# RWKV-7 recurrence and Wave-MLP mixer on one core: all transposes as 64-row halves into PSUM bank pairs, with merged evictions, products and stores, one bank pool and a new order

## The chip, the cores and the metric

One NeuronCore of a Trainium2 chip runs the kernel. Times are device microseconds of one execution. The kernel before has a median of 204.11 us over 3 runs (203.92 to 204.88). The engines are PE (TensorE, matmuls and transposes), ACT (ScalarE), DVE (VectorE), POOL (GpSimd) and SP (SyncE, which issues most transfers). Each engine runs its own instructions in a fixed order and waits on semaphores for the others.

## The reference

Four batches of 768 steps, 8 heads of 40 features (320 in all). First a recurrence over the steps, for each head, then a mixer over the whole sequence of a batch.

```python
for t in range(S):                       # state: [B, H, D, D]
    y[:, :, t] = einsum('bhd,bhde->bhe', rt, state)
    Sa = einsum('bhde,bhe->bhd', state, at)
    state = state * wt[:, :, None, :] - einsum('bhd,bhe->bhde', Sa, bt) \
            + einsum('bhd,bhe->bhde', vt, kt)
...
theta = x @ w_theta                      # x = y as [B, S, 320]
zr, zi = x * cos(theta), x * sin(theta)
y = einsum('ts,bsd->btd', w_tok_r, zr) + einsum('ts,bsd->btd', w_tok_i, zi)
u = x + y
out = u + maximum(u @ w_ch, 0.0)
```

## The kernel before, in words

**Tiles.** The steps are cut into 24 tiles of 128 steps, six to a batch, tile `i` of batch `i // 6`. A tile holds all 8 heads, as 4 pairs of heads padded from 40 to 64 features, so that a pair fills 128 columns (and, turned, 128 partitions).

**Preparation of a tile (`prep`).** SP loads w, k, b, a, v and r. ACT takes the logarithm of w (L426). PE sums it over the steps (`cs`, L436 and L439: the sums up to and with each step, and the tile's total per head); ACT takes the Exp (L443). The factor that leaves out the step itself comes in two ways: for the first 7 tiles from a second matmul and a second Exp (L449, L452), after that from an addition on DVE (`wi`, L455) and an Exp from SBUF (L460). k, b and a are multiplied by these factors, one `product` each (L409 on DVE, L410 on POOL). PE turns k and b (8 transposes of 128x128 into one PSUM bank), a (4) and v (4) with an identity as the moving operand (`transpose_pairs`, L373); ACT copies the result to SBUF as 32-bit words (L376) or DVE as 16-bit halves (L379). r, and v of the first 8 tiles, come in runs of eight steps for two tiles at a time (`turn_runs`, L504, L508).

**Scores.** Four sets per tile (`psi`, `phi`, `lamv`, `lamu`): 8 matmuls of 64 rows each (L532), two per head pair, into a pair of banks, then one eviction of 1024 columns with the triangular mask: on DVE (L542), or as an ACT copy (L544) and a POOL select (L546).

**Recurrence and readout.** `x0` (L573, L579), its copy `nx`, `nu` (L591) and its copy, both through ACT; then the new state `gt` (L612). For tiles 1 to 3 of the first batch PE adds the old state (L607) and DVE scales the sum (L631); from tile 4 on (`FROM_POOL = 4`) DVE adds (L623) and POOL scales (L627). The state and `nu` are turned by PE as well. `y` (L718 to L727) is scaled by DVE into `x` (L734).

**Mixer.** `theta` turns x of two tiles (L656), multiplies by `w_theta` (L688, and L698 for the 64 features left of each tile, both tiles side by side), and copies each tile's theta by ACT (L753). `sines` makes cosine and sine by ACT (L773) and one product each, `zr` and `zi` (L787 on DVE, L788 on POOL). `mix_row` adds up 12 matmuls a tile (L801) over the token weights, which were turned by PE earlier (L869, L874, L876); DVE adds x (L808). `channels` turns u, multiplies by `w_ch`, and DVE makes the output (L824), which SP stores tile by tile (L827). For a second tile of a pair the two weights are needed shifted by 64 rows; PE makes these copies by shifted identities in `wide` (L847, evicted at L851).

**Order and PSUM.** Every step is added to a plan with `add`. The order of all 1614 steps is the list `ORDER`; `HOMES` gives each PSUM result its bank; `PICK` names the steps that go to their second engine. Four of the eight banks form two pairs (`ps_d`), used for the scores; the other four are single banks (`ps_s`), used for all else. `WARM` puts 45 idle matmuls at the start (L920). A matmul that uses 64 rows and one that uses 128 are different row modes of PE.

Of the kernel before, what the change touches and what calls it, by code (L numbers as in the profile page):

```python
# [18 lines left out]
DOUBLE = 4  # L19
FROM_POOL = 4  # L20
EXCLUSIVE = 7
RUNS = 8
ORDER = [
# [184 lines left out]
def kernel(  # L208
# [52 lines left out]
    def paired(t):  # L261
        return t.rearrange("p (g c) d -> p g c d", c=2)
# [418 lines left out]
    def mixed(kind, q, lhs, wt, wkeys, lkey, at="tile"):  # L681
# [11 lines left out]
        if alone(q):  # L693
            return
# [263 lines left out]
```

## Time and profile before

| | |
|---|---|
| runs | 203.92, 204.11, 204.88 us |
| the profiled execution's span | 206.2 us |
| PE matmuls: instructions, busy | 3355, 193.7 us |
| DVE, ACT, POOL busy | 171.0, 154.3, 135.4 us |
| transferred | 30.82 MB, mean 149 GB/s |
| scores' masked eviction on DVE (L542) | 86 of 1217 to 1220 ns |
| the same as an ACT copy (L544), with a POOL select (L546) | 10 of 1023 to 1044 ns, 10 of 1087 to 1091 ns |
| transposes' evictions on ACT, 256 and 512 words (L376) | 375 to 386 and 590 ns |
| transposes' evictions on DVE, 512 and 1024 halves (L379) | 420 and 688 ns |
| Exp: 328 columns (L443), and the second one (L452, L460) | 24 of 454 ns, and 7 of 442, 17 of 476 ns |
| product of 320 columns on POOL (L410) and on DVE (L409) | 814 to 865 ns, 484 to 488 ns |

Busy time of an engine counts each moment once, so where successive instructions overlap it is less than count times mean. Matmuls are pipelined: one takes a latency of 180 to 300 ns, but the next starts long before it ends, so a busy PE can hold more or less work. The granted clock is given as a share of full speed; in this execution it is 1.00 in every stretch. "<-" with an engine and a line after an idle time names what ended it.

### The profile page before, as it was taken

The page shows a single profiled execution, that of the slowest core. Times are in us where ns is not written, and L with a number is a line of the kernel's source. Part 1 is how long each engine was busy: PE and PEld are TensorE (multiplying, and loading weights), DVE is VectorE, ACT ScalarE, POOL GpSimd, SP SyncE. Part 2 cuts the span into 40 slices and gives each one's busy share as a digit, 9 for nine tenths or more (in the row PEclk, how much of TensorE's full clock was granted, in tenths as well). Part 3 has the DMA queues.
Part 4 walks back from the last instruction along what each step waited for, and adds up shares of the span by engine and source line. Part 5 has one row for each costly group of instructions (what it writes and reads, how often), then busy time and mean ns, then how long its engine had stood idle before and what let it go on. Part 6 is the DMA issues. An engine that isn't in the chain of part 4 may idle for free. (4 is left out here: it accounts for less than half of the span.)

```text
span 206.2 us, 8107 instructions
## 1 busy us (share of the span) xinstructions
PE 193.7 (94%) x3355; PEld 155.8 (76%) x3355; DVE 171.0 (83%) x267; ACT 154.3 (75%) x345; POOL 135.4 (66%) x200
## 2 busy tenths in 40 slices
PE   6798999989898999999989999999999999999993
PEld 6586877877786788778768787989788877876761
DVE  4369988979998999799888889999999988867353
ACT  3377888879998989998877678799998955784001
POOL 8318545859896999687449949675399891339100
PEclk9999999999999999999999999999999999999999
DMA  6989977988999999999999799979898010100222
GB/s 107 212 139 242 168 132 152 189 150 195 185 193 167 185 164 186 199 164 217 166 234 157 149 197 168 170 161 185 166 199 213 15 59 5 64 3 33 99 95 95
DMA packets 127013, 30.82 MB, mean 149 GB/s; under 512 B 117632, under 2 KB 126976, under 8 KB 126976
## 3 DMA queue, kind: packets, MB, share of 16 engines
q1 hardware_dynamic: 124544, 27.54, 67.1%
q0 software_dynamic: 2432, 2.77, 8.4%
q8 instruction: 26, 0.43, 0.9%
q14 instruction: 11, 0.09, 0.2%
HBM read 29.13 MB, written 3.93 MB: 160 GB/s over the span
## 5 line engine op out<-in xcount | busy, mean ns | idle before, releaser
L410 POOL TENSOR_TENSOR kb<-raw_kb,ex 128x320 bf16<-128x320 f32 x46 | 36.9, 814 | 19.3 <-ACT ex L443 6.9
L801 PE MATMUL ps_s<-zr,wtok_r 128*128 128x320 bf16 x144 | 40.8, 299 | 1.0 <-ACT wtok_r L876 1.0
L801 PE MATMUL ps_s<-zi,wtok_i 128*128 128x320 bf16 x144 | 40.7, 299 | 0.0
L542 DVE TENSOR_TENSOR phi<-ps_d,mask_n 128x1024 bf16<-128x1024 f32 x23 | 28.0, 1218 | 5.1 <-PE ps_d L532 5.0
L542 DVE TENSOR_TENSOR psi<-ps_d,mask_p 128x1024 bf16<-128x1024 f32 x23 | 28.1, 1220 | 2.4 <-PE ps_d L532 1.4
L542 DVE TENSOR_TENSOR lamu<-ps_d,mask_p 128x1024 bf16<-128x1024 f32 x23 | 27.9, 1218 | 2.5 <-PE ps_d L532 1.7
L788 POOL TENSOR_TENSOR zi<-cs,xp 128x320 bf16<-128x320 f32 x21 | 16.6, 802 | 10.0 <-ACT cs L773 10.0
L410 POOL TENSOR_TENSOR ah<-raw_a,we 128x320 bf16<-128x320 f32 x23 | 19.9, 865 | 4.7 <-DMA raw_a<-in_a_dram 1.8
L542 DVE TENSOR_TENSOR lamv<-ps_d,mask_p 128x1024 bf16<-128x1024 f32 x17 | 20.6, 1217 | 1.5 <-PE ps_d L532 1.4
L801 PEld LDWEIGHTS <-wtok_r 128*128 128x128 bf16 x144 | 14.0, 97 | 5.7 <-ACT wtok_r L876 1.2
L532 PE MATMUL ps_d<-aT,kbT 64*128 64x128 bf16 x384 | 17.1, 221 | 0.5 <-ACT aT L376 0.5
L788 POOL TENSOR_TENSOR zr<-cs,xp 128x320 bf16<-128x320 f32 x19 | 15.3, 820 | 2.3 <-ACT cs L773 2.3
L373 PE MATMUL ps_s<-wide,kb 128*128 128x128 bf16 x192 | 15.7, 223 | 1.1 <-POOL kb L410 1.0
L801 PEld LDWEIGHTS <-wtok_i 128*128 128x128 bf16 x144 | 14.1, 98 | 3.6
L627 POOL TENSOR_TENSOR gt<-sum,ex 128x320 bf16<-128x320 f32 x13 | 9.6, 737 | 10.3 <-DVE sum L623 7.6
L508 ACT COPY rT<-ps_s 128x512 bf16<-128x512 bf16 x24 | 13.4, 598 | 3.1 <-PE ps_s L504 1.8
L808 DVE TENSOR_TENSOR up<-ps_s,xp 128x320 bf16<-128x320 f32 x22 | 10.6, 487 | 5.8 <-PE ps_s L801 5.7
L532 PEld LDWEIGHTS <-kbT 64*128 64x128 bf16 x384 | 12.5, 96 | 3.3 <-issue 1.3
L725 PE MATMUL ps_s<-kb,lamv 128*128 128x40 bf16 x192 | 14.8, 180 | 0.0
L727 PE MATMUL ps_s<-kb,lamu 128*128 128x40 bf16 x192 | 14.7, 179 | 0.0
L443 ACT ACTIVATE ex<-ps_s 128x328 f32<-128x328 f32 x24 | 10.9, 454 | 4.4 <-PE ps_s L439 3.1
L373 PEld LDWEIGHTS <-kb 128*128 128x128 bf16 x192 | 11.9, 99 | 3.0 <-POOL kb L410 1.6
(168 smaller groups left out, 600.3 us busy)
## 6 DMA issues: line engine op xcount, KB each, us to landing
raw_w<-in_w_dram SPq DMA_DIRECT2D x24, 160.0 KB, 4.2
raw_kb<-in_b_dram SPq DMA_DIRECT2D x24, 160.0 KB, 4.0
raw_kb<-in_k_dram SPq DMA_DIRECT2D x24, 160.0 KB, 3.8
raw_a<-in_a_dram SPq DMA_DIRECT2D x24, 160.0 KB, 4.2
raw_v<-in_v_dram SPq DMA_DIRECT2D x24, 160.0 KB, 3.7
raw_r<-in_r_dram SPq DMA_DIRECT2D x24, 160.0 KB, 3.9
out_dram<-oo SPq DMA_DIRECT2D x24, 160.0 KB, 1.9
wrow_i<-in_moe_w_tok_i_dram POOLq DMA_DIRECT2D x6, 192.0 KB, 5.9
```

What stands on the lines that cost most here:

```text
L373: nc.tensor.transpose(out=dst[:, c:c + 128], in_=pair(src, g), identity=ident)
L410: pool = ("POOL", lambda: nc.gpsimd.tensor_tensor(out=dst, in0=in0, in1=in1, op=ALU.mult))
L443: got = add("ACT", "exp", i, lambda: nc.scalar.activation(out=ex.rearrange("p h x -> p (h x)"), in_=ps(pk)[:, 0:DM + 8], func=AF.Exp), 440 ...
L508: add("ACT", "e" + nm, i + x, lambda x=x, dst=dst: nc.scalar.copy(out=dst.rearrange("p (g t q) -> p g t q", g=G, q=8), in_=ps(pr).bitcast( ...
L532: nc.tensor.matmul(t[:, q, g, :], lhsT=lhs[rows(q), g * 128:(g + 1) * 128], rhs=rhs[rows(q), g * 128:(g + 1) * 128], start=True, stop=True)
L542: add("DVE", kindm, i, lambda: nc.vector.tensor_tensor(out=flat, in0=whole(), in1=mask.to_broadcast([128, 2 * G, 128]), op=ALU.mult), 1217 ...
L627: add("POOL", "wgt", i, lambda: nc.gpsimd.tensor_tensor(out=new_state, in0=sum_t, in1=wm.to_broadcast([128, 8, D]), op=ALU.mult), 830, [(" ...
L725: nc.tensor.matmul(o, lhsT=lamv[:, p, g, :], rhs=kb[:, 0, h, 0:D], start=first, stop=False, skip_group_check=True)
L727: nc.tensor.matmul(o, lhsT=lamu[:, p, g, :], rhs=kb[:, 1, h, 0:D], start=False, stop=True, skip_group_check=True)
L788: pool = ("POOL", lambda: nc.gpsimd.tensor_tensor(out=dst, in0=in0, in1=in1, op=ALU.mult))
L801: nc.tensor.matmul(ps(pk)[:, 0:DM], lhsT=wtok[nm][:, s, j * 128:(j + 1) * 128], rhs=zs[c][:, s], start=n == 0 and c == 0, stop=n == NT - 1 ...
L808: add("DVE", "uadd", q, lambda: nc.vector.tensor_tensor(out=u, in0=ps(pk)[:, 0:DM], in1=x, op=ALU.add), 488, [pk, x_key(q)], [u_key(q)], a ...
```

## The change

- **Transposes.** Each 128x128 transpose becomes two of 64 rows (`turn`), one for the upper and one for the lower half of the partitions, with a 64x64 part of the identity, into the two banks of a pair. One eviction reads both banks (`turned`). A tile's k, b, a and (from tile 8) v are turned together, 12 or 16 blocks, with one eviction into `feat` in place of two or three.
- **Exp.** Both sums of a tile are made by PE in a bank pair, the second from `lw` shifted by one element (`LEAD`), and one Exp of 2x328 makes both factors; `wi`, `we` and `sx` are gone.
- **Products.** k and b in one product of 640 columns, cosine and sine likewise; every product may now go to DVE or POOL. On DVE: 13 of k and b, 10 of a, 11 of z. On POOL: 11, 14, 13.
- **Mixer.** Theta's four matmuls of two tiles are one step with one copy of 640 columns; output, and store, of two tiles likewise. The shifted weights are loaded a second time instead of made by PE (four more transfers). The token weights are one tile per block, turned and evicted together.
- **State.** `FROM_POOL` 4 to 24: all states are joined by PE and scaled by DVE.
- **PSUM.** One pool of four bank pairs; a single result takes one half of a pair.
- **Order.** New `ORDER`, `HOMES` and `PICK` (1350 steps instead of 1614); of the scores' evictions 26 instead of 10 go to ACT and POOL; `WARM` is 32 instead of 45. The constants of the start are made in another sequence.

The instructions as built:

| | before | after |
|---|---|---|
| PE matmuls | 3355 | 4244 |
| of these transposes | 882 of 128 columns | 1764 of 64 columns, 64 rows |
| DVE, ACT, POOL steps of the plan | 242, 335, 174 | 211, 277, 107 |
| loads and stores issued by SP | 144 and 24 | 144 and 13 |

```diff
-FROM_POOL = 4
+FROM_POOL = 24
...
-WARM = {21: 32, 28: 4, 30: 2, 41: 7}
+WARM = {21: 32}
...
+    ex_t = sb("ex", [128, 2, H, D + 1], FP32, NEX)
+    feat_t = sb("feat", [128, 16, 128], BF16, NTR)
...
-    doubles = [psum.tile([128, 2, 512], FP32, name=f"ps_d{i}") for i in range(DOUBLE // 2)]
-    singles = [psum.tile([128, 512], FP32, name=f"ps_s{i}") for i in range(BANKS - DOUBLE)]
+    doubles = [psum.tile([128, 2, 512], FP32, name=f"ps_{i}") for i in range(BANKS // 2)]
...
     def ps(key):
         h = plan.home[key]
-        return doubles[h[0] // 2] if len(h) == 2 else singles[h[0] - DOUBLE]
+        t = doubles[h[0] // 2]
+        return t if len(h) == 2 else t[:, h[0] % 2]
...
-    def transpose_pairs(dst, srcs):
-        for j, src in enumerate(srcs):
-            for g in range(G):
-                c = (j * G + g) * 128
-                nc.tensor.transpose(out=dst[:, c:c + 128], in_=pair(src, g), identity=ident)
...
+    def turn(dst, blocks):
+        for n, src in enumerate(blocks):
+            for h in range(2):
+                nc.tensor.transpose(out=dst[:, h, n * 64:n * 64 + 64], in_=src[rows(h)],
+                                    identity=ident[rows(h), rows(h)])
...
+    def turned(kind, kinde, i, blocks, skeys, dst, dkeys, at="tile", eng="ACT"):
...
+        def words():
+            nc.scalar.copy(out=dst.bitcast(FP32).rearrange("p n (a w) -> p a n w", a=2),
+                           in_=ps(p)[:, :, 0:32 * n].rearrange("p a (n w) -> p a n w", w=32))
...
+        def halves():
+            nc.vector.tensor_copy(
+                out=dst.rearrange("p n (a w) -> p a n w", a=2),
+                in_=ps(p).bitcast(BF16)[:, :, 0:64 * n].rearrange("p a (n w) -> p a n w", w=64))
...
+            before = lw[:, LEAD - 1:LEAD - 1 + H * 64].rearrange("p (h x) -> p h x", x=64)
+            nc.tensor.matmul(t[:, 1, 0:DM + 8], lhsT=mask_p[:, 0, :], rhs=before[:, :, 0:D + 1],
+                             start=True, stop=True)
...
+        add("ACT", "exp", i, lambda: nc.scalar.activation(
+            out=ex.rearrange("p a h x -> p a (h x)"), in_=ps(pk)[:, :, 0:DM + 8], func=AF.Exp),
+            730, [pk], [kex], table="lnexp")
...
-        for j, nm in enumerate("kb"):
-            product("kb", i, paired(kb[:, j])[:, :, :, 0:D], paired(raw_kb[s4][:, j]), invW,
-                    [("raw_" + nm, s4), kex], [("kb", j, i % NKB)], fast)
+        product("kb", i, kb[:, :, :, 0:D], raw_kb[s4],
+                ex[:, 0:1, :, 0:D].to_broadcast([128, 2, H, D]),
+                [("raw_k", s4), ("raw_b", s4), kex], [("kb", i % NKB)], fast)
...
+        blocks = [pair(t, g) for t in (kb[:, 0], kb[:, 1], ah) for g in range(G)]
+        skeys, dkeys = [("kb", i % NKB), ("ah", i % 3)], [("feat", st)]
+        if i >= RUNS:
+            blocks += [pair(vb, g) for g in range(G)]
...
+        turned("tt", "et", i, blocks, skeys, feat[:, 0:len(blocks)], dkeys)
...
+            x = x_of(q).rearrange("p (a d) -> p a d", a=1).to_broadcast([128, 2, DM])
+            product("z", q, z[:, :, j], cs_t[j // 3][:, :, j % 3], x,
+                    [("cs", j // 3, 0, j % 3), ("cs", j // 3, 1, j % 3), x_key(q)],
+                    [("z", bi % 2, j)], fast)
...
+            add("ACT", "eth2", q, lambda: nc.scalar.copy(
+                out=th_t[:, j:j + 2], in_=ps(pk)[:, :, 0:DM]), 700, [pk],
+                [("th", j), ("th", j + 1)])
...
+                      (dst[rows(1), 2, :], src[0:64, :]),
+                      (dst[:, 3:5, :], src[64:320, :].rearrange("(a p) d -> p a d", p=128)))
```

More of the change, by code (lines that the diff above doesn't have):

```diff
@@ L367, in pair, with by_halves @@
         return t[:, 2 * g:2 * g + 2, :].rearrange("p a b -> p (a b)")
-    def transpose_pairs(dst, srcs):
-        for j, src in enumerate(srcs):
-            for g in range(G):
-                c = (j * G + g) * 128
-                nc.tensor.transpose(out=dst[:, c:c + 128], in_=pair(src, g), identity=ident)
-    def copy_words(out, in_):
-        nc.scalar.copy(out=out.bitcast(FP32), in_=in_)
-    def copy_halves(out, in_):
-        nc.vector.tensor_copy(out=out, in_=in_.bitcast(BF16))
-    def evac(eng, kind, i, psk, dst, n, reads=(), writes=()):
-        act = ("ACT", lambda: copy_words(dst, ps(psk)[:, 0:n // 2]))
-        dve = ("DVE", lambda: copy_halves(dst, ps(psk)[:, 0:n // 2]))
-        one, two = (act, dve) if eng == "ACT" else (dve, act)
-        add(eng, kind, i, one[1], n, [psk], writes, alts=(two,))
+    def turn(dst, blocks):
[3 more added lines that the diff above has]
+                                    identity=ident[rows(h), rows(h)])
+    def by_halves(n):
+        return dict(mode=64, tail=tail(64), cost=2 * n * mm(64) / 2)
+    def turned(kind, kinde, i, blocks, skeys, dst, dkeys, at="tile", eng="ACT"):
+        p = ("ps", kind, i)
+        n = len(blocks)
+        add("PE", kind, i, lambda: turn(ps(p).bitcast(BF16), blocks), reads=skeys, writes=[p],
+            at=at, new=(p, 2), **by_halves(n))
+        def words():
[5 more added lines that the diff above has]
+                in_=ps(p).bitcast(BF16)[:, :, 0:64 * n].rearrange("p a (n w) -> p a n w", w=64))
+        alts = [("ACT", words), ("DVE", halves)]
+        if eng == "DVE":
+            alts.reverse()
+        add(alts[0][0], kinde, i, alts[0][1], n * 128, [p], dkeys, at=at, alts=(alts[1],))
     def loads(i):
@@ L411, in product @@
         one, two = (dve, pool) if fast else (pool, dve)
-        add(one[0], kind, i, one[1], 0, reads, writes, alts=(two,) if i < 8 or i >= N - 2 else ())
+        add(one[0], kind, i, one[1], 0, reads, writes, alts=(two,))
     def cast(kind, i, dst, src, reads, writes, fast):
@@ L480, in prep @@
[L480 to L485 removed]
+        st = i % NTR
+        feat = feat_t[st]
+        blocks = [pair(t, g) for t in (kb[:, 0], kb[:, 1], ah) for g in range(G)]
@@ L745, in theta @@
         src = xs_t[q % 2] if alone(q) else xp_t[q // 2 % (NX // 2)]
[L746 to L754 removed]
+        blocks = blocks_of(src)
+        turned("xt", "ext", q, blocks, sorted({x_key(q), x_key(i)}),
+               xT_t[n][:, 0:len(blocks)], [("xT", n)])
+        mixed("th", q, xT_t[n], wth, [("wth", c) for c in range(4)], ("xT", n))
+        if i == N - 1:
+            return
+        pk, j = ("ps", "th", q), q % NCH
+        if alone(q):
+            add("ACT", "eth", q, lambda: nc.scalar.copy(
+                out=th_t[:, j], in_=ps(pk)[:, 0:DM]), 427, [pk], [("th", j)])
+        else:
+            add("ACT", "eth2", q, lambda: nc.scalar.copy(
+                out=th_t[:, j:j + 2], in_=ps(pk)[:, :, 0:DM]), 700, [pk],
+                [("th", j), ("th", j + 1)])
     def sines(bi, js):
@@ L778, in sines @@
         for j in js:
-            for c in range(2):
-                fast = bi == B - 1 and j == NT - 1
-                z = (zr_t, zi_t)[c][bi % 2]
-                q = bi * NCH + j
-                product_z(i, z[:, j], cs_t[j // 3][:, c, j % 3], x_of(q),
-                          [("cs", j // 3, c, j % 3), x_key(q)], [("z", c, bi % 2, j)], fast)
-    def product_z(i, dst, in0, in1, reads, writes, fast):
-        dve = ("DVE", lambda: nc.vector.tensor_tensor(out=dst, in0=in0, in1=in1, op=ALU.mult))
-        pool = ("POOL", lambda: nc.gpsimd.tensor_tensor(out=dst, in0=in0, in1=in1, op=ALU.mult))
-        one, two = (dve, pool) if fast else (pool, dve)
-        add(one[0], "z", i, one[1], 0, reads, writes, alts=(two,))
+            fast = bi == B - 1 and j == NT - 1
+            z, q = z_t[bi % 2], bi * NCH + j
+            x = x_of(q).rearrange("p (a d) -> p a d", a=1).to_broadcast([128, 2, DM])
+            product("z", q, z[:, :, j], cs_t[j // 3][:, :, j % 3], x,
+                    [("cs", j // 3, 0, j % 3), ("cs", j // 3, 1, j % 3), x_key(q)],
+                    [("z", bi % 2, j)], fast)
     def mix_row(bi, j):
@@ L795, in mix_row, with chunk @@
         x, u = x_of(q), u_of(q)
-        zs = (zr_t[bi % 2], zi_t[bi % 2])
-        order = list(range(NT))
-        for n, s in enumerate(order):
-            def chunk(s=s, n=n):
-                for c, nm in enumerate("ri"):
-                    nc.tensor.matmul(ps(pk)[:, 0:DM],
-                                     lhsT=wtok[nm][:, s, j * 128:(j + 1) * 128],
-                                     rhs=zs[c][:, s], start=n == 0 and c == 0,
-                                     stop=n == NT - 1 and c == 1)
-            need = [("z", 0, bi % 2, s), ("z", 1, bi % 2, s), ("wtok", "r", j), ("wtok", "i", j)]
-            add("PE", "row", q, chunk, 2 * mm(320), need, [pk], at="row",
-                new=(pk, 1) if n == 0 else None, tail=tail(320))
+        z = z_t[bi % 2]
+        for s in range(NT):
+            def chunk(s=s):
+                for c in range(2):
+                    nc.tensor.matmul(ps(pk)[:, 0:DM], lhsT=wtok[j][:, c, s, :],
+                                     rhs=z[:, c, s], start=s == 0 and c == 0,
+                                     stop=s == NT - 1 and c == 1)
+            add("PE", "row", q, chunk, 2 * mm(320), [("z", bi % 2, s), ("wtok", j)], [pk],
+                at="row", new=(pk, 1) if s == 0 else None, tail=tail(320))
         add("DVE", "uadd", q, lambda: nc.vector.tensor_tensor(
@@ L836, in mixer_weights @@
                     out=to, in_=part), 580, [], [(key, c)], at="rel",
-                    work=260 if c else 1030)
-            up, down = wide[:, 128:256], wide[:, 0:128]
-            moves = ((((up, 0), (down, 1)), 3, slice(0, 128), 3),
-                     (((up, 1), (down, 2)), 4, slice(0, 128), 4),
-                     (((down, 0),), 2, rows(1), 2))
-            for terms, slot, part, c in moves:
-                p = ("ps", "w" + key, c)
-                def go(terms=terms, p=p, dst=dst):
-                    for m, (lhs, at) in enumerate(terms):
-                        nc.tensor.matmul(ps(p)[:, 0:DM], lhsT=lhs, rhs=dst[:, at, :],
-                                         start=m == 0, stop=m == len(terms) - 1)
-                add("PE", "wo", 10 * n + c, go, len(terms) * mm(320), [(key, 0), (key, 1)], [p],
-                    new=(p, 1), tail=tail(320), at="rel")
-                copies = [(e, lambda f=f, p=p, dst=dst, slot=slot, part=part: f(
-                    out=dst[part, slot, :], in_=ps(p)[part, 0:DM]))
-                    for e, f in (("ACT", nc.scalar.copy), ("DVE", nc.vector.tensor_copy))]
-                add("ACT", "ewo", 10 * n + c, copies[0][1], 425, [p], [(key, c)], at="rel",
-                    alts=(copies[1],))
@@ L857, in wtok_block @@
+                    work=260 if c in (1, 2) else 1030)
     def wtok_block(tb):
         i = 7 + tb
[L859 to L878 removed]
@@ new lines, in wtok_block @@
+        row = wrow[tb % 2]
+        for c, ap in enumerate((moe_w_tok_r, moe_w_tok_i)):
+            add("POOL", "wdma", 2 + tb, lambda c=c, ap=ap: nc.gpsimd.dma_start(
+                out=row[:, c], in_=ap[tb * 128:(tb + 1) * 128, :]), 580, [],
+                [("wrow", c, tb % 2)], at="rel", work=1240)
+        blocks = [row[:, c, s * 128:(s + 1) * 128] for c in range(2) for s in range(NT)]
+        turned("wt", "ewt", i, blocks, [("wrow", 0, tb % 2), ("wrow", 1, tb % 2)],
+               wtok[tb].rearrange("p c s b -> p (c s) b"), [("wtok", tb)])
```

339 lines of the change are left out of this document (133 added, 206 removed), and 213 rows, old and new, of tables (HOMES, ORDER, PICK).

## The prediction

> **What bounds the kernel now.** I read the head of the page first, then the stretches of ten microseconds, then the chain of waits, and last the groups and the order of time for prices.
>
> ```profile
> span 206.2 us, 8107 instructions
> PE 193.7 (94%) x3355; PEld 155.8 (76%) x3355; DVE 171.0 (83%) x267; ACT 154.3 (75%) x345; POOL 135.4 (66%) x200
> ```
>
> One core, four loaded engines. PE's 94% says little alone, since pipelined matmuls count as busy through their latency. The stretches say when it is full:
>
> ```profile
> 50.00:60.00 10.00, 9.17 (x203) 7.66 (x198) 9.52 (x13) 9.94 (x23) 9.01 (x14) 1.00 1.00 178
> 130.00:140.00 10.00, 10.00 (x231) 8.83 (x225) 9.80 (x14) 8.93 (x23) 7.06 (x10) 1.00 0.90 166
> 170.00:180.00 10.00, 10.00 (x175) 8.04 (x172) 8.43 (x14) 6.09 (x14) 2.72 (x4) 1.00 0.10 35
> 190.00:200.00 10.00, 10.00 (x80) 6.98 (x79) 4.39 (x10) 0.42 (x1) 1.64 (x2) 1.00 0.24 84
> ```
>
> The columns are the stretch, then PE, PEld, DVE, ACT and POOL busy, granted clock, DMA share and GB/s. Early on everything is busy and PE is not quite full; DMA stands at 0.80 to 1.08 until 160 us and falls to 0.1 after it. Late, PE is full and the others have room. The chain of waits confirms it:
>
> ```profile
> 105.98 0.72 PE ps_s L801 x4
> 107.28 0.55 PE ps_d L532 x16
> ...
> 188.79 5.81 PE ps_s L801 x42
> ...
> 199.00 2.02 PE ps_s L801 x14
> 203.03 0.49 DVE oo L824
> ```
>
> From 106 us to the end the chain is PE's own instruction stream with no foreign wait in it: there PE time is kernel time. Before 106 us it is a mixture of loads and ACT, DVE and PE in turn. So I price the change in two parts, cut at the Exp of tile 15 (it starts at 110.8 us).
>
> PE's pace comes from the order of time (start, length of the run, count):
>
> ```profile
> 58.37 0.36 PE L591 MATMUL ps_s<-nx,phi 128*128 128x40 bf16 x8
> 58.66 0.31 PE L698 MATMUL ps_s<-wth,xT 64*128 64x320 bf16 x2
> 58.80 0.39 PE L532 MATMUL ps_d<-rT,nuT 64*128 64x128 bf16 x8
> 59.88 0.39 PE L373 MATMUL ps_s<-wide,nu 128*128 128x128 bf16 x4
> ```
>
> A run lasts one latency plus (count-1) paces. Full transposes (L373, one 219 ns): (390-219)/3 = 57, 56 ns by the exact starts. 40 columns (L591): (360-180)/7 = 25. The score matmuls (L532) use 64 rows each; the starts come in pairs 4 ns apart, the pairs 56 ns apart, so two halves of the array run side by side. 320 columns take 136. By columns: N/2.4 + 2.5 ns, not under 25. A change between 128-row and 64-row work costs 95 ns more than the pace (58.37 plus eight paces is 58.57, L698 starts at 58.66); the way back costs 96. Over the built instruction order, before has 168.0 us of matmul paces and 125 such changes, 12.0 us: 180.0 of 206.2.
>
> **The change, part by part.**
>
> *Transposes in halves.* 882 full transposes x 56 ns = 49.2 us go; 1764 halves of 64 columns come. No trace row shows a 64-row matmul of 64 columns. Lower bound: pairs side by side as in L532, 64/2.4 + 2.5 = 29 ns a pair, 25.7 us in all. Upper bound: the 25 ns of L591 holds for each instruction of both halves, 50 ns a pair, 44.1 us. I take 29, because L532 is the nearest row (64 rows, two banks) and starts its second half after 4 ns, not 25: gain 23.5 us. The Trainium skill, TensorE: Matmul & The Clock Gate, section "Back-to-back issue gap", gives a floor of about 25 ns for every matmul of up to 64 columns, which speaks against this; by it the sum would be the upper bound. By the pairs of L532 the floor does not hold across the two halves, so trace and rule differ there.
>
> *Row-mode changes.* Each transpose block is now 64-row work among 128-row work: the built order counts 199 changes, 74 more, x 96 ns = +7.1 us.
>
> *Smaller PE terms.* The shifted copies of the two mixer weights are loaded, not made by PE: 10 x 136 = -1.4. Warm-up 45 to 32: -0.7 by the 56 ns pace; these run in the start's waits, and what that cover is worth if the clock rises later is some 107-56 ns on the few dozen matmuls up to 13 us, under 2 us. The second cumulative sum by PE on 17 more tiles, 139 each: +2.4. Joining the state by PE instead of POOL on 13 tiles, 136 each: +1.8. PE in all: -23.5 + 7.1 - 1.4 - 0.7 + 2.4 + 1.8 = -14.3, from 180.0 to 165.7.
>
> *ACT.* Exp: 24x454 + 7x442 + 17x476 = 22.1 us becomes 24 of 656 columns, 454 + 328x0.83 = 727 each, 17.4. One eviction per tile (1024 words, about 1010 by the 0.82 ns a word between 256 and 512 words of L376) stands for two or three. Theta by pairs. But 26 score evictions at 1030 stand where 10 stood: +16.5. Summed over the built order with the rows' durations, 179.7 becomes 178: nothing.
>
> *DVE.* 16 score evictions (1218 each) and 17 adds (L455, 485) go, -27.7; k and b in one product of 640 (488 + 320x1.04 = 821), 13 of them, 10 a-products, 11 z-products of 640: +24.6, less the 8 such products of before (4.7). Paired outputs save 1.6, copies 1.3. 184.4 becomes about 173.
>
> *The port.* Those 34 products read two SBUF tiles, and so do POOL's. Here the trace has a warning, the order of time around one of the five z-products that DVE does now:
>
> ```profile
> 68.81 0.95 DVE L787 TENSOR_TENSOR zr<-cs,xp 128x320 bf16<-128x320 f32 x1
> 67.87 1.55 POOL L788 TENSOR_TENSOR zr<-cs,xp 128x320 bf16<-128x320 f32 x2
> 69.40 1.77 POOL L788 TENSOR_TENSOR zi<-cs,xp 128x320 bf16<-128x320 f32 x2
> ```
>
> DVE's product starts inside a POOL product and takes 953 ns instead of 482; the POOL product that then starts inside it takes about 1.0 instead of 0.8. The five took 953, 480, 555, 482 and 811: 175 ns over 482 on average. Price: 34 x 0.175 = 6 us on DVE; bounds 0 and 34 x 0.47 = 16. The Trainium skill, SBUF — State Buffer, section "Who interferes with whom", says that a two-input DVE instruction and a GpSimd read lock each other out for a whole instruction; the trace agrees.
>
> *POOL and SP.* POOL loses 13 state products, half of its k and b products and ten z-products' worth of work, gains 16 selects (1.09 each) and four weight loads (0.7 each to issue). These stand in POOL's queue among the products of the first tiles, so the product behind each comes 0.7 later and PE's transposes wait for it; the first part is not PE's, and its cover is that products run a tile ahead; without it 4 x 0.7 = 3 us. The constants of the start are reordered; tile 0's Ln waits for its load until 3.8 us anyway. POOL's sum: 142 to about 110. Its products of 640 are in no row: between the cast of 640 (0.73) and two of 320 (1.63); I take 1.55, nearer the two, since both have two inputs. SP's loads are the same 144, reordered to run further ahead (102 instead of 92 ahead of tile 15's Exp); the stores become 13 instead of 24, which shortens what a late store holds up behind it.
>
> **The sum.** By tile 15's Exp the built order holds, before and after: PE 87.2 and 90.1 us with its changes; ACT 77.3 and 83.4; DVE 86.1 and 88.9 (each duration less the overlap with the next: 104 ns on ACT, 84 on DVE); POOL 69 and 58. None has less to do but POOL, and DMA's share averages 0.96 over these 110 us. So the first part gains nothing; 22 of the 34 products lie in it, 22 x 0.175 = 4 us on DVE, of which I put 3 on the path: 110.8 + 3 = 114. After it PE has 73.8 instead of 90.3 us. Before, the remaining 95.4 us held 90.3 of PE and 5.1 of waits and last eviction and store. After: 73.8 + 5.1, plus 2 because DVE (63.6 + 2 of lock) now comes near PE: 81. Span 195. The profiled span, 206.2, is 2.1 above the median of the runs, 204.11, so **193** is forecast.
>
> **Rivals.**
>
> 1. *The port lock decides (other side).* Place: DVE's queue, where a late product holds the score evictions behind it, these hold bank pairs, and PE waits for a pair, of which there are now four for everything. For: 953 ns; POOL is over half busy. Against: three of five were hardly touched. At the full 0.47, 22 x 0.47 = 10 in the first part and 6 in the second, plus about 4 of PE waits at the pairs: 110.8 + 10 + 73.8 + 5.1 + 10 = 210, 208 measured. It outweighs the gain of 14 from about 0.4 us a product on.
>
> 2. *Halves don't overlap.* 50 ns a pair: PE +18.4, 8.3 of it after the cut (73.8 of 163.9), and about half of the other 10 on the path: 195 + 8 + 5 = 208, 206 measured.
>
> 3. *Everything arrives.* The first part shrinks to its DMA time (0.96 x 110.8 = 106) and the lock costs nothing: 106 + 79 = 185, 183 measured. For: the join takes a POOL step of 0.74 out of the state's chain on 13 tiles. Against: ACT and DVE have more to do there.
>
> 4. *No gain that shows* (the change frees PE, but not the time): the first part slips by ACT's 6 and DVE's 7 together, 124, and the second by pairs waiting for 1.2 us evictions, 83: 207, 205 measured.
>
> **How the numbers follow.** Forecast 0.57, rival 1 0.16, rival 2 0.09, rival 3 0.12, rival 4 0.06. The forecast's own range is 187 to 200 (first part -4 to +6, second -2 to +3). The range reaches to 185 and 207, which leaves out most of rival 3 and the far end of 1. A measurement can tell 0.5%, 1 us (the runs spread from 203.92 to 204.88). Faster: 0.57 + 0.12 = 0.69 and 0.01 of rival 4; same: most of 4 and a little of 2, 0.07; slower: 0.23.
>
> **What would show it.** Transposes (L344): runs at 29 ns a pair, or 50. The DVE products of 640: mean near 0.95 (0.82 + 0.13 to 0.18), or over 1.2. Tile 15's Exp near 114 us. PE full from there on, with 74 us of paces. Selects of POOL near 1.09. I am wrong in kind if PE shows idle time released by DVE in the second part, or if the paired evictions read from two banks take much longer than their words say.

## The result

The changed kernel takes 237.02 us (median of 4 runs, 235.98 to 239.28) where the kernel before takes 204.5 (203.92 to 205.08): 1.160 times as long, 95% interval 1.153 to 1.167. Forecast were 193, so the sign was wrong. The profiled executions span 237.6 and 206.2 us. An execution more than 1.5% above the fastest of the same kernel is in a slower state and is left out of all medians, ranges and ratios below; with all four of its executions, experiment 1 has a median of 218.1 us, the number that later expectations use.

The head of the page of the changed kernel, with the row of granted clock and that of the transfers' share, in 40 slices of 5.9 us:

```profile
span 237.6 us, 9707 instructions
...
PE 192.2 (81%) x4244; PEld 145.0 (61%) x4244; DVE 174.6 (73%) x238; ACT 159.3 (67%) x285; POOL 106.8 (45%) x130
...
PEclk9999999976999979999999999999999999999998
DMA  6998899979989985226329998898898400002122
```

No engine is full any more. PE's busy share fell from 94% to 81%, DVE's from 83% to 73%, and none of the others rose. The stretches (the columns as in the prediction) say the same of the late part, where before had PE at 10.00 of 10:

```profile
50.00:60.00 10.00, 9.15 (x188) 6.74 (x181) 6.19 (x5) 6.35 (x14) 5.02 (x7) 0.66 1.11 206
110.00:120.00 10.00, 9.27 (x148) 6.75 (x148) 6.80 (x8) 5.91 (x11) 6.40 (x7) 1.00 0.51 67
130.00:140.00 10.00, 8.75 (x205) 6.53 (x203) 7.80 (x11) 7.01 (x13) 2.59 (x3) 1.00 0.99 188
170.00:180.00 10.00, 8.05 (x225) 6.31 (x225) 7.20 (x11) 8.35 (x15) 4.67 (x7) 1.00 0.97 183
190.00:200.00 10.00, 7.92 (x175) 6.10 (x176) 8.41 (x12) 5.53 (x9) 5.07 (x5) 1.00 0.01 2
```

The chain that ended last, in order of time, was PE alone after 106 us in the kernel before. Now it goes from engine to engine:

```profile
193.06 0.43 ACT nx L543
...
195.48 1.19 DVE kb L391
196.67 0.41 DVE gt L589
...
199.93 0.50 DVE xp L680
...
200.45 0.43 ACT nx L543
...
200.93 0.37 PE ps L549 x8
...
201.32 0.45 ACT nu L553
...
204.14 1.03 ACT phi L500
```

So PE got its smaller work and then waited. The written order with the prediction's prices gives PE 146.4 us of paces and 199 row-mode changes, 19.0 us: 165.4 against 180.0 before, 14.6 less. What PE loses beyond that between its first and its last matmul (idle time, with what a lowered clock adds; called the stall from here) rose from 21.7 to 67.1 us, 45.4 more. 45.4 less 14.6 is 30.8, nearly all of the 31.4 by which the spans differ: the loss is stall. By place: the Exp of tile 15 starts at 138.50 us instead of 110.76, 27.7 later, and what comes behind it takes 99.1 instead of 95.4. The two Exp in the order of time, before and after:

```profile
110.76 0.44 ACT L443 ACTIVATE ex<-ps_s 128x328 f32<-128x328 f32 x1 [0.48 <-PE ps_s L439]
```

```profile
138.50 0.72 ACT L426 ACTIVATE ex<-ps 128x656 f32<-128x656 f32 x1
```

What PE and the rest wait for is told by the waits, of which these are four (engine, tile and line; what ended the wait; us in total, times, longest):

```profile
DVE up L750 <- PE ps L745: 7.5, 9, 2.1
...
ACT nx L543 <- PE ps L537: 5.2, 6, 2.8
...
PE ps L532 <- DVE xp L680: 3.3, 2, 2.8
...
ACT nx L543 <- DVE xp L680: 3.0, 3, 1.2
```

The last line has no sense by the data. `nx` (L543) copies `x0` of one tile from PSUM; `xp` (L680) scales `y` of another tile from PSUM; neither reads what the other writes. The order of time shows one such place, where the two lie in different banks (start, length, engine, line; in brackets the idle time and its releaser):

```profile
171.06 0.21 PE L537 MATMUL ps<-v,psi 128*128 128x40 bf16 x2
...
171.30 0.49 DVE L680 TENSOR_TENSOR xp<-ps,ex 128x320 bf16<-128x320 f32 x1
...
171.88 0.42 ACT L543 CAST nx<-ps 128x320 bf16<-128x320 f32 x1 [1.24 <-DVE xp L680]
...
172.35 0.36 PE L549 MATMUL ps<-nx,phi 128*128 128x40 bf16 x8 [0.52 <-ACT nx L543]
```

The `x0` of tile 19 (L537) is done at 171.27. Its copy starts only at 171.88, right after `xp` of tile 17 has ended at 171.79, and PE then stands idle for 0.52 us until the copy is there. By `HOMES` the `x0` lies in bank 2 and the `y` in bank 3: the two halves of one pair, thus of one PSUM tile `ps_1`. In the compiled program `nx` waits on a semaphore of DVE there. Such waits, on an instruction that touched only the other bank of the same tile, are 108 in the changed program and none in the one before, where a single result had a tile of its own. So the framework orders the accesses of different engines to a PSUM tile by the whole tile, two reads included. Not all 108 are needless: 30 of them involve a result that takes both banks (in 11, a copy of `r` out of one bank waits for the last transpose, which fills the other). The Trainium skill, PSUM — Partial Sum Buffer, section "PSUM bank collisions raise a hardware error", asks only that accesses be guarded by bank; by that rule the other 78 waits are not needed. Experiment 1 runs without them, in 216.3 us instead of 237.0.

That is theory F (shared tiles): the waits across banks cost most of the loss. Its rivals were A (a store that waits at the head of SP's queue holds the loads behind it), C (the new order itself, with long evictions and products in it) and E (halves of transposes and their mode changes); later L (DVE's and POOL's products hold each other up, and the bank pairs themselves). Several expectations below speak of a replay: an estimate made by running through the written order with the durations, waits and overlaps of the traces. It gives 204 us for before, 236 for after, and 214 for after without these waits.

### The profile page after: what moved, and what is told of

Read it like the earlier page. It is cut to its first block, busy times and chain, and to the rows that moved or that the text cites. A ratio compares the mean times of both kernels' runs of the same rounds, so it can differ in the third digit from the quotient of the medians.

```text
span 237.6 us, 9707 instructions
## 1 busy us (share of the span) xinstructions
PE 192.2 (81%) x4244; PEld 145.0 (61%) x4244; DVE 174.6 (73%) x238; ACT 159.3 (67%) x285; POOL 106.8 (45%) x130
## 5 line engine op out<-in xcount | busy, mean ns | idle before, releaser
L745 PE MATMUL ps<-z,wtok 128*128 128x320 bf16 x288 | 48.1, 299 | 9.1 <-ACT nx L543 2.5
L745 PEld LDWEIGHTS <-wtok 128*128 128x128 bf16 x288 | 25.7, 97 | 20.6 <-issue 11.2
L498 DVE TENSOR_TENSOR psi<-ps,mask_p 128x1024 bf16<-128x1024 f32 x20 | 24.3, 1221 | 8.8 <-PE ps L490 6.1
L498 DVE TENSOR_TENSOR lamu<-ps,mask_p 128x1024 bf16<-128x1024 f32 x22 | 26.7, 1216 | 2.3 <-PE ps L490 2.1
L392 POOL TENSOR_TENSOR kb<-raw_kb,ex 128x640 bf16<-128x640 f32 x11 | 15.7, 1428 | 22.0 <-ACT ex L426 13.7
L357 ACT COPY feat<-ps 128x1024 f32<-128x1024 f32 (+1 forms) x18 | 17.0, 943 | 12.5 <-PE ps L344 12.5
L490 PEld LDWEIGHTS <-feat 64*128 64x128 bf16 x576 | 19.8, 100 | 8.1 <-issue 3.0
L392 POOL TENSOR_TENSOR z<-cs,xp 128x640 bf16<-128x640 f32 x12 | 18.4, 1552 | 11.4 <-ACT cs L724 11.3
L490 PE MATMUL ps<-feat 64*128 64x128 bf16 x384 | 18.9, 228 | 3.2 <-ACT feat L357 1.6
L426 ACT ACTIVATE ex<-ps 128x656 f32<-128x656 f32 x24 | 17.3, 722 | 2.6 <-PE ps L422 2.1
L502 POOL TENSOR_SCALAR_AFFINE_SELECT phi<-phi 128x1024 bf16<-128x1024 bf16 x10 | 11.9, 1194 | 15.5 <-ACT phi L500 15.4
L543 ACT CAST nx<-ps 128x320 bf16<-128x320 f32 x24 | 10.2, 425 | 12.6 <-PE ps L537 5.2
L498 DVE TENSOR_TENSOR phi<-ps,mask_n 128x1024 bf16<-128x1024 f32 x14 | 17.1, 1219 | 1.4 <-PE ps L490 1.1
L680 DVE TENSOR_TENSOR xp<-ps,ex 128x320 bf16<-128x320 f32 x22 | 10.7, 486 | 6.5 <-PE ps L674 2.4
```

Of the source, the lines that this page charges most:

```text
L357: nc.scalar.copy(out=dst.bitcast(FP32).rearrange("p n (a w) -> p a n w", a=2), in_=ps(p)[:, :, 0:32 * n].rearrange("p a (n w) -> p a n w", ...
L392: pool = ("POOL", lambda: nc.gpsimd.tensor_tensor(out=dst, in0=in0, in1=in1, op=ALU.mult))
L426: add("ACT", "exp", i, lambda: nc.scalar.activation(out=ex.rearrange("p a h x -> p a (h x)"), in_=ps(pk)[:, :, 0:DM + 8], func=AF.Exp), 73 ...
L490: nc.tensor.matmul(t[:, q, g, :], lhsT=lhs[rows(q), g, :], rhs=rhs[rows(q), g, :], start=True, stop=True)
L498: add("DVE", kindm, i, lambda: nc.vector.tensor_tensor(out=flat, in0=whole(), in1=mask.to_broadcast([128, 2 * G, 128]), op=ALU.mult), 1217 ...
L502: add(None, "sel", i, None, 0, [dkey], [dkey], alts=(("POOL", lambda: nc.gpsimd.affine_select(out=flat, in_=flat, pattern=[[0, 2 * G], [1, ...
```

## The experiments

Four executions were timed of each; ratios are against the kernel before on the same chip, with their 95% interval.

**1. The same program without the waits across banks.** The instructions, their order, engines and banks stay; the declared independence removes waits between different banks of a pair.

```diff
+    held = {}
+
+    def apart(o, made):
+        for key in dict.fromkeys(o.writes + o.reads):
+            banks = plan.home.get(key)
+            if banks is None:
+                continue
+            users = held.setdefault(banks[0] // 2, [])
+            if len(banks) == 2 and o.new is not None:
+                users.clear()
+            for ins in made:
+                for other, was in users:
+                    if not set(other) & set(banks) and was.engine != ins.engine:
+                        tc.declare_no_dep(ins, was, reason="other bank")
+            users.extend((banks, ins) for ins in made)
...
+            traced = nc.cur_bb.bb.instructions
+            start = len(traced)
             o.fn()
+            apart(o, nc.cur_bb.bb.instructions[start:])
```

> The changed kernel with the same instructions, order and banks, but without the waits between two uses that lie in different banks of one pair. The compiled program of the changed kernel has 108 waits in which the instruction waited for touches the other bank of the same PSUM tile; the kernel before has none. Theory F (shared tile): these waits are the main loss. Replaying the written order with the durations of the traces gives 236 us with them and 214 us without, so this runs at 210 to 218 us. Theory A (a store at the head of SP's queue holds the loads up): unchanged at about 237 us, or at most 3 us less. Theory C (the order itself is too long) and E (the 64-row halves): about 237 us.

Measured: 216.3 us (216.08 and 216.52), ratio 1.056 [1.053, 1.059]: 20.7 us less than the changed kernel. The 30 waits that involve a result in both banks are still in it. Its profiled execution spans 218.0 us; the head of its page and four lines of its waits:

```profile
span 218.0 us, 9715 instructions
...
PE 188.1 (86%) x4244; PEld 141.8 (65%) x4244; DVE 175.4 (80%) x238; ACT 158.2 (73%) x285; POOL 107.4 (49%) x130
```

```profile
ACT nu L553 <- PE ps L549: 4.7, 7, 1.3
...
DVE up L750 <- PE ps L745: 4.0, 4, 1.8
...
ACT nx L543 <- PE ps L537: 3.7, 7, 1.2
...
DVE xp L680 <- ACT nx L543: 0.3, 1, 0.3
```

`nx`, `nu` and L532 no longer wait for `xp` at all, `up` waits 4.0 instead of 7.5 us for its matmuls, and PE's stall is 47.6 instead of 67.1 us. The 19.5 us of stall are the 19.6 by which the two profiled spans differ. Tile 15's Exp starts at 127.82: 10.7 of the gain lie ahead of it, the rest behind.

**2. The kernel before, with shared tiles put in.** The other way round: of the old kernel only the four single banks are made halves of two tiles.

```diff
-    singles = [psum.tile([128, 512], FP32, name=f"ps_s{i}") for i in range(BANKS - DOUBLE)]
+    halved = [psum.tile([128, 2, 512], FP32, name=f"ps_s{i}") for i in range((BANKS - DOUBLE) // 2)]
+    singles = [t[:, c] for t in halved for c in range(2)]
```

> The kernel before with nothing changed but the PSUM tiles: its four single banks become the halves of two tiles of two banks, with every bank, instruction and place in the order as it was. Theory F: slower by far, since the single banks carry most uses here; the same replay gives 204 us as it is and 329 us with the tiles shared, so well over 250 us. Theories A, C and E: 204.5 us, unchanged, because no instruction, order or transfer differs.

Measured: 350.85 us, 1.71 times the 204.87 of before (without an interval). The profiled execution spans 360.0 us; two lines of its page's head and its row of clock:

```profile
span 360.0 us, 8105 instructions
...
PE 253.1 (70%) x3355; PEld 190.0 (53%) x3355; DVE 176.1 (49%) x267; ACT 163.2 (45%) x345; POOL 135.6 (38%) x200
...
PEclk9569655655599899758989899989697589969897
```

No bank, instruction or place in the order is different; only the tiles are, and the time rises by 146 us. The compiled program has 369 waits on the other bank of a tile, where before has none. By the replay the waits alone make 329; the granted clock, 0.80 on average in the profiled execution, is not in it. So F is shown both ways: the waits taken out, and put in.

**3. A store held at the head of SP's queue.** In the changed kernel two stores of the first batch's outputs (the pairs of tiles 0 and 2) stand ahead of loads of tiles 14 to 17, and the queue waits. Two entries of `ORDER` are moved behind load step 764.

```diff
-    ..., 382, ..., 402, ..., 764, ...
+    ..., 764, 382, 402, ...
```

> The changed kernel with the first two paired stores moved in SP's queue behind the 14 loads of the tiles 14 to 17 that stood behind them, to the last place that their buffer allows. Theory A: the loads of tiles 14 and 15 start 31 us earlier, the Exp of tile 15 comes some 20 us earlier (138 to about 118 us) and the time falls to 215 to 220 us. Theory F: SP's wait was long but nobody was waiting for what stood behind it; 237 us within 2 us, with the loads early and the Exp of tile 15 where it was.

Measured: 240.27 us (239.0 to 242.17), ratio 1.174 [1.167, 1.180]. SP's longest wait, in the changed kernel and then here:

```profile
SPq L776 <- DVE oo L773: 75.1, 7, 31.1
```

```profile
SPq L776 <- DVE oo L773: 73.2, 9, 27.7
```

The load of tile 15's w is issued at 96.17 instead of 128.00 us, and its Exp starts no earlier, at 138.93 instead of 138.50:

```profile
138.93 0.72 ACT L426 ACTIVATE ex<-ps 128x656 f32<-128x656 f32 x1
```

A wait of 31 us was the longest of SP's queue, and taking it from ahead of these loads brings nothing (the time is 3 us longer): theory A falls. What is late there is late for another reason.

**4 and 5. Full transposes, with the waits and without.** The changed kernel, and experiment 1, with 128-row transposes written one after the other, evicted as before in one instruction.

```diff
-            for h in range(2):
-                nc.tensor.transpose(out=dst[:, h, n * 64:n * 64 + 64], in_=src[rows(h)],
-                                    identity=ident[rows(h), rows(h)])
+            nc.tensor.transpose(out=dst[:, n // 8, n % 8 * 128:n % 8 * 128 + 128], in_=src,
+                                identity=ident)
```

> The changed kernel with its transposes as 128-row blocks again (one instruction of 128x128 for two halves) into the same bank pairs; the evictions read contiguous words, the order stays. Theory E (the halves and their mode changes cost more than they save): faster than 237 us, by up to the 7 us of the added mode changes. Theory F: the halves did what was forecast for them (TensorE's paces fell to 146 us), so undoing them adds about 23 us of paces less 7 us of mode changes, of which the replay puts 10 us on the path: 243 to 250 us.

> e1_banks_apart with the transposes as 128-row blocks again, as in e4. What the halves are worth where no false wait hides it. If they give the forecast (23 us of paces less 7 us of mode changes) on the path: 229 to 236 us against 218 us; the replay gives 226 us. If TensorE is not what the time hangs on here: 218 us within 2 us. Theory E (the halves cost more than they save): under 216 us.

Measured: 247.03 us (246.22 to 248.33), ratio 1.207 [1.202, 1.211], and 226.75 (225.85 to 227.5), ratio 1.109 [1.104, 1.113]. So halves are worth 10.0 us with the waits and 10.5 without: E falls, they are a gain. The order built here has 178 mode changes, against 199: only 21 of the 74 additional ones come from halves, the rest from the order. PE's work is 21.7 us more in full transposes (169.95 + 17.1 against 146.4 + 19.0); of this some 10 reach the time; for the rest the stall is smaller.

**6 and 7. A new order, knowing the waits or without them.** The same instructions on the same engines; `ORDER` and `HOMES` come from a search with the replay, for the changed kernel (6) and for experiment 1 (7). The lists begin so (7 below):

```diff
-    0, 20, 21, 22, 1, 2, 3, 23, 24,
+    0, 7, 20, 156, 8, 1, 21, 6, 27,
```

> The changed kernel with another written order and other home banks alone, searched by a replay that holds an access to a pair until the last access to either of its banks has ended; all waits on shared tiles stay. Theory F: the waits cost what the order makes of them; the replay gives 203 us, so 200 to 211 us. If the order cannot be told from the waits (theory C, an order made for other durations, without the shared tiles): it would gain as much as e5 does, not less. If four pairs are simply too few banks: 230 us or more whatever the order.

> e1_banks_apart (no waits between different banks of a pair) with another written order and other home banks; every instruction, its engine and its operands as in the changed kernel. The order was searched with the replay of the traces' durations, which gives 214 us for the order of the change and 198 us for this one. Theory F with the order as the second cause: 195 to 206 us, so that what was left of the loss in e1 (218 us) was the written order. Theory L (what is left is the port lock and the bank pairs themselves): 214 to 220 us, since the same products run on VectorE beside the same GpSimd work.

Measured: 222.52 us (221.45 to 224.54), ratio 1.089 [1.083, 1.096], for the shared tiles; 226.85 (225.47 to 227.28), ratio 1.108 [1.103, 1.113], for the banks apart, which is worse than the order it replaced. Both miss their numbers. The replay left the loads of weights out of the DMA's work; in the second one the DMA's share is 1.00 on average up to 110 us. That this is why both missed is likely, not shown. Still, the first shows that 14.5 of the 32.5 us go with an order that knows the waits, while all tiles stay shared; and four pairs are not too few banks as such, for which 230 us or more were expected.

**8. New order and engines, banks apart.** As 7, with `PICK` also searched.

> As e5, but the search may also move a product, cast, eviction or mask between the two engines that the kernel has for it. Replay: 191 us. Theory F with the order: 188 to 200 us, which would be faster than the kernel before (204.5 us). Theory L: not under 204 us.

Measured: 218.62 us (218.32 to 220.72), ratio 1.072 [1.066, 1.078], a miss too, with a mean clock of 0.911 in the profiled execution.

**9 to 11. The search with a better replay** (all transfers, the lock of DVE and POOL, the clock): for banks apart, for the kernel before, and for the changed kernel with its shared tiles.

> As e7 (no waits between different banks of a pair, order, banks and choice of engine searched again), with a replay that also holds a VectorE product and a GpSimd operation apart, lets the weight loads share the DMA engines, and halves TensorE's clock after a window of 3.4 us with less than 0.56 of it busy, as the traces so far show. That replay gives 219 us for e1 (measured 218), 216 us for e7 (219.7) and 241 us for the changed kernel (237); for this order it gives 192 us. If the shared tiles, the lock and the clock are all that held the new instructions back: 190 to 200 us, faster than the kernel before. If something is missing in that account (as in e5, replayed 217, measured 227): over 204 us.

> The kernel before with an order, banks and engines searched in the same way and for as long; no other edit. The replay gives 205 us for the kernel before as it is and 196 us for this order. It tells how much of a gain in e10 is the search and how much the change's instructions: if the change's instructions are worth their 14 us of TensorE time, e10 is some 10 us under this one; if both end within 5 us of each other, the instructions of the change bring little even without the waits on shared tiles, and what e10 gains is the order.

> The changed kernel with its shared tiles and all their waits, order, banks and engines searched with the same replay, which holds each access to a pair until the last access to either bank has ended. Replay: 241 us for the order of the change, 196 us for this one. Theory F: the loss came from an order that did not know of these waits, so most of it is recovered, 195 to 208 us. If the waits cannot be ordered around on the chip (because each delay moves the next): over 215 us, as in e6 (222.5).

| | us | range | ratio |
|---|---|---|---|
| banks apart | 207.6 | 206.21 to 208.77 | 1.013 [1.007, 1.020] |
| before's instructions | 206.89 | 206.53 to 208.25 | 1.014 [1.008, 1.020] |
| shared tiles | 213.75 | 212.12 to 215.21 | 1.044 [1.037, 1.050] |

The replays were 192, 196 and 196, so the search believes too much; it does not even reach the order that the kernel before has. But under the same search, with one order found for each, both sets of instructions end at the same time: taken together, what the change does to the instructions neither gains nor loses anything that is seen here. Order and engines alone, with the shared tiles and 99 waits across banks left, bring back 23.3 of the 32.5 us; 213.75 lies between the two outcomes expected for it.

**12 and 13. The products.** Experiment 1 with 27 products on the other engine, and with every merged product again as two of 320 columns. The edit of 13:

```diff
+        parts = [(dst, in0, in1)] if kind == "ah" else [
+            (dst[:, c], in0[:, c], in1[:, c]) for c in range(2)]
+
+        def each(engine):
+            for to, x, y in parts:
+                engine.tensor_tensor(out=to, in0=x, in1=y, op=ALU.mult)
```

> e1_banks_apart with 27 of the two-input products moved between VectorE and GpSimd (14 to VectorE, 13 to GpSimd) and nothing else: order, banks and all other steps as in e1. They are chosen with the replay so that products of the two engines meet less. In e1 the 34 products on VectorE take 13 us more than the same products do alone. Theory L (the lock holds part of what e1 still loses): 209 to 214 us (replay 212, against 219 for e1), with the products on VectorE close to 0.82 and 0.49 us. If the lock is hidden behind other work: 218 us within 1.5 us.

> e1_banks_apart with each merged product (k with b, cosine with sine; 640 columns) issued as two instructions of 320 columns on the same engine, one behind the other. Alone, two of 320 cost 0.07 to 0.1 us more on VectorE (2 x 0.49 less an overlap of 0.08, against 0.82) and 0.2 us more on GpSimd (2 x 0.81 against 1.42) than one of 640. If the length of the merged products is what costs (a product on one engine holds the other's back until it ends, now up to 1.4 us instead of 0.8): under 215 us, and the excess of VectorE's products falls from 13 us to 7 us or less. If it is not: 218 to 222 us, the price of the longer GpSimd work.

Measured: 221.2 us (219.99 and 222.47), ratio 1.083 [1.074, 1.092], and 218.95 (218.45 to 220.01), ratio 1.072 [1.068, 1.076]. Both are slower than experiment 1, by 4.9 and 2.7 us, and the first meets neither of its expectations. By what DVE's products take beyond the time that they take undisturbed (0.82 us for 640 columns, 0.488 for 320), experiment 1 loses 13.2 us to POOL, the moved ones 11.4, the split ones 14.8. The length of the merged products is therefore not the cost; what the lock costs the kernel is not told apart, since moving the products hardly changed what DVE loses, and the time rose.

**14. The clock.** Experiment 1 with idle matmuls ahead of the places where the granted clock fell.

```diff
-WARM = {21: 32}
+WARM = {21: 32, 42: 4, 470: 4, 491: 8, 1146: 20}
```

> e1_banks_apart with 36 idle matmuls more, in four places where TensorE waits (before the second scores of tile 0, the turn of r of tile 8, the state of tile 7 and theta of tile 18), chosen with the replay. In e1 the granted clock fell to half in 10 us at the start and in two windows of 3.4 us later, each after a window with TensorE busy for less than 0.56. If the clock is a main part of what is left: 213 to 216 us (replay 214.5 against 218.5), with a granted clock above 0.975 instead of 0.961. If not: 218 us within 1 us, or more where the fillers delay their own operation.

Measured: 216.69 us (215.06 to 216.71), ratio 1.058 [1.053, 1.063]; the mean clock is 0.976 instead of 0.961 in the profiled executions. Experiment 1 has 216.3 and 1.056: no gain is seen. Either the clock is no main part of what is left, or the idle matmuls cost what they bring.

## Why the prediction was wrong

**The step that failed** is the sum's last one, "After: 73.8 + 5.1, plus 2", and with it "So the first part gains nothing ... 110.8 + 3". Both take PE's and the others' waits over from the kernel before, though the change gives every single result a half of a shared tile. The diff shows that line, `return t if len(h) == 2 else t[:, h[0] % 2]`, and the prediction put no price on "one bank pool": neither a bound from below nor from above. Rival 1 did look at the pairs, "of which there are now four for everything", but as room, not as a cause of waits between two results that both have their room. The price was 20.7 us in this order (experiment 1), and the order made it dear: one searched with these waits in view takes 14.5 us less with all tiles shared (experiment 6). By place, the sum has 114 us up to tile 15's Exp and 81 behind it; the spans show 138.5 and 99.1, and 127.8 and 90.2 without the waits.

**What is left.** Experiment 1 is 11.8 us over before. PE's work there is 14.6 less, its stall 47.6 against 21.7, 25.9 more. Order and choice of engines take 8.7 of the 11.8 away (experiment 9). So C, the order, has a part in the rest, though the same search does not find the order of the kernel before either (206.89 for its 204.5). Which part the lock has is open; a higher clock alone took nothing off (experiment 14).

**PE.** Halves run at 29 ns a pair: sixteen (eight pairs) take 0.41 us, one latency of about 0.2 and seven paces of 0.029.

```profile
171.19 0.41 PE L344 MATMUL ps<-ident,kb 64*128 64x64 bf16 x16
```

The lower bound was right, and the floor of about 25 ns that the Trainium skill, TensorE: Matmul & The Clock Gate, section "Back-to-back issue gap", states for up to 64 columns does not hold across the two halves, which start 3 to 4 ns apart here. The change in PE's work, -14.3 forecast, is -14.6. But the 74 mode changes were laid to the halves, and 53 of them are the order's.

**The other engines' prices.** The groups by form (count | busy us, mean ns | idle before, releasers) hold the rows that were missing:

```profile
L391 DVE TENSOR_TENSOR z<-cs,xp 128x640 bf16<-128x640 f32 x10 | 12.6, 1269 | 2.1 <-ACT cs L724 2.1
L391 DVE TENSOR_TENSOR kb<-raw_kb,ex 128x640 bf16<-128x640 f32 x13 | 12.5, 962 | 2.0 <-ACT ex L426 2.0
...
L357 ACT COPY feat<-ps 128x1024 f32<-128x1024 f32 x12 | 12.2, 1013 | 9.3 <-PE ps L344 9.2
...
L391 DVE TENSOR_TENSOR ah<-raw_a,ex 128x320 bf16<-128x320 f32 x10 | 10.3, 1033 | 2.4 <-ACT ex L426 1.5 <-DMA raw_a<-in_a_dram 0.9
```

The eviction of 1024 words takes 1013 ns (1010 forecast), Exp of 656 columns 722 (727), POOL's product of k and b 1428 and of z 1552 (1550), its selects 1092 to 1194 (1090). On DVE k and b take 962 (950 forecast) but z 1269 instead of 950, and a 1033 instead of 663 (488 + 175). Together 13 x 0.141 + 10 x 0.545 + 10 x 0.448 = 11.8 us more than undisturbed, put down to POOL; 6 was taken, 16 was the upper bound.

**Rivals.** None reaches 237; the dearest, the lock's, gave 208. The course of rival 4 is the one that was seen, the first part late (138.5 us for its 124) and PE's gain lost behind it (99.1 for 83), but its causes, ACT's 6 and DVE's 7 us and waits for pairs, are not the ones found. The sign named for being wrong in kind, "idle time released by DVE in the second part", is there: from 138.5 us on PE's matmuls wait 6.7 us for DVE, in a dozen places. That stores "become 13 instead of 24, which shortens what a late store holds up" was wrong (31.1 us of wait at the head of the queue), but cost nothing (experiment 3).

## What to carry to other kernels

When a diff puts two results into one tile, list which instructions of other engines now follow each other on that tile, and price each of them, even where addresses and banks are apart; the waits of the compiled program, counted before and after, tell it without a run. A gain on the engine that bounds a kernel holds only as far as the next chain between engines lets it: here 21.7 us of PE work gave some 10. The longest wait in a profile need not cost anything, and only moving it tells.

## What the runs showed of the hardware

**The granted clock falls with a half-idle PE, not only an idle one.** Stretches of 3.4 us of the changed kernel (clock third from the end):

```profile
47.60:51.00 3.40, 1.61 (x54) 1.21 (x50) 2.46 (x3) 2.13 (x6) 1.93 (x3) 1.00 0.64 109
51.00:54.40 3.40, 3.00 (x67) 2.33 (x65) 2.34 (x2) 2.58 (x6) 2.36 (x4) 0.50 1.06 172
54.40:57.80 3.40, 3.40 (x45) 2.15 (x46) 2.24 (x3) 1.99 (x3) 1.42 (x1) 0.50 1.16 205
57.80:61.20 3.40, 2.61 (x68) 2.13 (x66) 1.80 (x3) 2.01 (x5) 0.73 (x2) 0.99 0.95 214
```

PE is busy for 1.61 of 3.40 us and the clock is halved in the next stretch; 3.00 of 3.40 do not bring it back here, a full one does. After 57.80, with 2.61 of 3.40 busy, it stays full. So some 1.8 us of idle PE were followed by 6.8 us at half speed. Counted over the traces of all runs, in stretches of 3.41 us cut where the clock changes: none with PE busy under 0.52 of the stretch kept the full clock, none under 0.80 brought it back, and above 0.80 some did not (one of 0.97). The Trainium skill, TensorE: Matmul & The Clock Gate, section "What's actually happening", has the halving after an idle window of 3.4 us; here a window with PE busy 47% was enough.

**DVE's and POOL's products shut each other out by whole instructions.** Two pieces of the order of time:

```profile
114.59 0.82 DVE L391 TENSOR_TENSOR z<-cs,xp 128x640 bf16<-128x640 f32 x1
...
117.42 2.02 DVE L391 TENSOR_TENSOR z<-cs,xp 128x640 bf16<-128x640 f32 x1
```

```profile
117.36 3.33 POOL L392 TENSOR_TENSOR z<-cs,xp 128x640 bf16<-128x640 f32 x2 [3.60 <-ACT cs L724]
```

The same product takes 0.82 us alone and 2.02 where it starts 0.06 us behind one on POOL. A longer product holds the other engine up for longer in one place, but in sum the length is not what costs: with the products split in two, DVE lost 14.8 us instead of 13.2 (experiment 13).
